# Routed attention and a gated FFN on one core: a fifth group prepared by VectorE, v loaded four heads ahead, one-hots issued by GpSimd

## The chip, the cores and the metric

One Trainium2 chip, one core. The metric is the device time of one execution in microseconds (us): the median of twelve runs, beside one profiled execution whose trace is read here. The engines are PE (TensorE, matrix products), VectorE (DVE in the profile), ScalarE (ACT), GpSimd (POOL) and SyncE (SP, which here only issues DMAs). Each engine runs its own list of instructions in order and waits on semaphores for the others.

## What is computed

Attention in which a query sees only the keys of its own cluster, then a gated FFN behind an RMS norm. There are 4 batches, 8 heads, 768 positions, a head dimension of 64 and 16 clusters for each head; the FFN takes 3072 tokens of 512 to 1536 and back.

```python
q_assign = np.argmax(np.einsum('bhsd,hcd->bhsc', q_n, c_n), axis=-1)
k_assign = np.argmax(np.einsum('bhsd,hcd->bhsc', k_n, c_n), axis=-1)
mask = q_assign[:, :, :, None] == k_assign[:, :, None, :]
scores = scale * np.matmul(q, k.transpose(0, 1, 3, 2))
scores = np.where(mask, scores, -1000000000.0)
scores = scores - np.max(scores, axis=-1, keepdims=True)
attn = np.exp(scores)
attn = attn / (np.sum(attn, axis=-1, keepdims=True) + 1e-09)
return np.matmul(attn, v).astype(np.float32)
...
rms = np.sqrt(np.mean(x * x, axis=-1, keepdims=True) + 1e-06)
xn = x / rms * rms_g
g = xn @ w_gate
silu = g * (1.0 / (1.0 + np.exp(-g)))
val = xn @ w_val
return (silu * val @ w_out).astype(np.float32)
```

## The kernel before

**The mask as part of the product.** Each head's q and k are held transposed in SBUF, 64 rows of values, and under them 16 rows that hold a one-hot of the position's cluster. The product of the two (line 345) is then the score plus a large number where the clusters agree, and the exponential with a bias (line 349) brings all others to 0. The large number is `ZS`: up to group 4 the keys are divided by it and the exponential multiplies it back; from group `BG` on the keys stay as they are and their one-hots are multiplied by it (line 282).

**Groups.** The 32 heads (4 batches of 8) are prepared in eight groups of four, numbered 0 to 7. Preparing a group means:

- `load_qk` and `load_v` (lines 95 and 100): DMAs on SP's queue into the staging buffers. There are `NQ` = 6 for q and k and `NV` = 8 for v; a load waits until its buffer is free. For groups below `BG`, q or k of a head is one DMA of 192 KB (line 85). From `BG` on it is four DMAs of 48 KB (line 93), which bring half rows of 32 numbers (128 bytes) to such places that transposing blocks of 32 by 32 gives the layout needed.
- `trans` (line 209): below `BG`, three transposes by PE into PSUM (line 218), then a copy to `qkT` by ScalarE (line 224) or VectorE. From `BG` on, one block transpose by VectorE (line 214).
- `cast` (line 230): from `qkT` to bf16 in `qext` and `kext`. GpSimd casts q; k is cast by VectorE below `BG` and by GpSimd from `BG` on. `vcast` (line 239) is GpSimd's too, and frees the v buffer.
- `cluster_steps` (line 265): cluster products on PE (line 251), then the largest, the comparison and transposes on VectorE; the last, line 283, leaves the one-hots in `put`.
- `place` (line 289): DMAs of 12 KB each, which carry the one-hots to their rows under q and k.

**Units.** The attention runs in eight units: for each batch first one half of the queries, then the other. A unit has 24 rounds (8 heads, 3 rounds each) of scores on PE, exponential on ScalarE and, a round later, the product with v (line 363). Between the rounds `attention` (line 655) puts pieces of other work from a list: it spreads them by their costs, which are written beside each piece. In unit u this other work is the expert products (lines 441 and 466) of the units before, and the preparation of group u + 2. Unit 1 prepares groups 2 and 3, unit 2 prepares group 4 and ends what remains of group 3 (the one-hots of its keys), units 3 to 5 prepare groups 5 to 7. The batch of unit u uses groups 2(u // 2) and the next, so unit 2 uses groups 2 and 3.

**Order of the queues.** The order on each engine is the order in which the program writes the pieces. `others` (line 494) stands with each head n of groups 2 to 7: it casts v of head n, loads q and k of head n + 6, and loads v of head n + 8. Before it, `second_batch` (line 607) loads q and k of heads 12 and 13 and v of heads 8 to 15. At the end of a unit's norm, `rms` (line 403) puts a transposing DMA of the normed tokens, `xnT`, on SP's queue; the next expert products need it. The one-hots of group 2 are placed on SP's queue, all others on GpSimd's. In unit 1, GpSimd's list is: v casts of group 2, then casts and v casts of group 3 with the three loads of `w_out` (line 204, 512 KB each) between them, then the one-hots of group 3's queries.

The lines that set the work of a group above 3:

```python
if g > 3:
    a[:1] = [(1.4, lambda f=(a[0][1], a.pop(4)[1]): [x() for x in f])]
    a.append((0.0, lambda: [place(nc.gpsimd, g, m) for m in range(2)]))
```

Of the kernel before, what the change touches and what calls it, by code (L numbers as in the profile page):

```python
# [22 lines left out]
def kernel(  # L23
# [12 lines left out]
    nc = tc.nc  # L36
    B, H, S, D = q.shape
# [16 lines left out]
    CUT = 2 * FC - 8  # L54
    LEAD = 6
    NQ, NV = 6, 8
    BG = 5

    ctx.enter_context(tc.manual_schedule())
    pool = lambda n, b, **kw: ctx.enter_context(tc.tile_pool(name=n, bufs=b, **kw))  # L60
# [16 lines left out]
    def src(a, n):  # L77
        b, h = divmod(n, H)
        return a[b, h].rearrange("(p t) d -> p t d", t=ST)

    def load(n, part, on=None):
        if n not in staged:
            staged[n] = stage.tile([P, 2, ST, D], F32, tag="qk", name="qk")
        if n < BG * HG:
            (on or nc.sync).dma_start(out=staged[n][:, part], in_=src((q, k)[part], n))
# [9 lines left out]
    def load_qk(n):  # L95
        if n < B * H:
            load(n, 0)
            load(n, 1)

    def load_v(n, vq=None):  # L100
        if n >= B * H:
            return
        stagedv[n] = stage.tile([P, ST, D], F32, tag="vs", name="vs", bufs=NV)
        (vq or nc.sync).dma_start(out=stagedv[n], in_=src(v, n))
# [104 lines left out]
    def trans(g, h, part, on=None):  # L209
        if (g, h // 2) not in qkT:  # L210
            qkT[g, h // 2] = qk32.tile([P, 2, 2, UQ], F32, tag="qkT", name="qkT")
        qk = staged[g * HG + h]
        if g >= BG:
            nc.vector.transpose(qkT[g, h // 2][:, h % 2, part], qk[:, part].rearrange("p t d -> p (t d)"))
            return
        ps = ps_g.tile([P, UQ], F32, tag="gen", name="tq")
        for i in range(HT):
            nc.tensor.transpose(ps[:, i * P:(i + 1) * P], qk[:, part, 2 * i:2 * i + 2].rearrange("p t d -> p (t d)"),  # L218
                                ident_f)
        to, by = qkT[g, h // 2][:, h % 2, part], 1.0 / ZS if part else 1.0  # L220
        if on is nc.vector:
            nc.vector.tensor_scalar_mul(to, ps, by)  # L222
        else:
            nc.scalar.activation(to, ps, ACT.Copy, scale=by)
# [5 lines left out]
    def cast(on, g, h, part, es=(0, 1)):  # L230
        for e in es:
            to = cols((kext if part else qext)[g % 4][:D, h], g, e)
            of = qkT[g, h // 2][e * D:(e + 1) * D, h % 2, part]
            if on is nc.scalar:
                nc.scalar.copy(to, of)
            else:
                on.tensor_copy(to, of)  # L237

    def vcast(n):
        nc.gpsimd.tensor_copy(vbf[n // HG % 4][:, n % HG, :, :D], stagedv[n])  # L240
# [24 lines left out]
    def cluster_steps(g, m):  # L265

        of = {}

        def products():
            of["cl"] = cluster_products(g, [(h, m) for h in range(HG)])  # L270

        def most():
            of["mx"] = largest(of["cl"])

        def same():
            of["ohT"] = asg.tile([P, UQ], BF16, tag="ohT", name="ohT", bufs=2)
            compare(of["ohT"].rearrange("p (b e c) -> p b e c", e=2, c=NC), of["cl"], of["mx"])

        def back():
            put[g, m] = asg.tile([P, UQ], BF16, tag="oh", name="oh", bufs=3)  # L280
            if m and g >= BG:
                nc.vector.tensor_scalar_mul(of["ohT"], of["ohT"], ZS)
            nc.vector.transpose(put[g, m], of["ohT"])  # L283

        return [products, most, same, back]
# [3 lines left out]
    def place(on, g, m, es=(0, 1)):  # L289

        ext = (kext if m else qext)[g % 4]
        for h in range(HG):
            for e in es:
                on.dma_start(out=ext[D:D + NC, h, e * UQ:(e + 1) * UQ],  # L294
                             in_=put[g, m][32 * h + e * NC:32 * h + (e + 1) * NC])
# [39 lines left out]
    def scores(u, h, i):  # L335
# [12 lines left out]
        of = ps[:, :, :w] if nt == HT else flat[:, :n * w].rearrange("p (c w) -> p c w", w=w)  # L348
        nc.scalar.activation(pT[u, h][:, n * i:n * i + n, :w], of, ACT.Exp, bias=off, scale=scale if g >= BG else scale * ZS)  # L349

# [135 lines left out]
    def group_work(g):  # L486

        t, c = [], []
        for h in range(HG):
            n = g * HG + h  # L490
            w = 0.0 if g >= BG else 0.3
            t += [(w, lambda h=h: trans(g, h, 0)), (w, lambda h=h: trans(g, h, 1))]

            def others(n=n):
                vcast(n)
                load_qk(n + NQ)
                load_v(n + NV)

            def both(h=h, f=others):
                cast(nc.gpsimd, g, h, 0)  # L500
                f()
                cast(nc.gpsimd if g >= BG else nc.vector, g, h, 1, (0,))
            if g == 2:
                c.append((0.0, others))
            else:
                c += [(0.0, both), (0.0, lambda h=h: cast(nc.gpsimd if g >= BG else nc.vector, g, h, 1, (1,)))]
        a = []
        for m in range(2):
            a += [(0.0 if i else 0.7, f) for i, f in enumerate(cluster_steps(g, m))]
            if g == 3:  # L510
                a.append((0.0, lambda m=m: place(nc.gpsimd, g, m)))
            elif g == 2:
                a.append((0.0, (lambda: (place(nc.sync, g, 1), place(nc.sync, g, 0, (1,)))) if m else
                          (lambda: place(nc.sync, g, 0, (0,)))))
        if g > 3:
            a[:1] = [(1.4, lambda f=(a[0][1], a.pop(4)[1]): [x() for x in f])]
            a.append((0.0, lambda: [place(nc.gpsimd, g, m) for m in range(2)]))
        return t, c, a
# [5 lines left out]
    def group(g):  # L524

        if g >= NG:
            return [], []
        t, c, a = group_work(g)
        return [x for h in range(HG) for x in t[2 * h:2 * h + 2] + c[2 * h:2 * h + 2]], a
# [13 lines left out]
    def ffn_work(u):  # L543
        n = UNITS[u][2] / HT
        return [(0.64 * n, lambda f=f, val=val: gv(u, f, val)) for f in range(FC) for val in (False, True)]

    def out_work(u):
        return [(0.86, lambda t=t, p=p: out_mm(u, t, p)) for t in range(UNITS[u][2]) for p in range(3)]
# [58 lines left out]
    def second_batch():  # L607
        nc.sync.dma_start(out=hold, in_=invs[0].rearrange("p a t -> p (a t)"))
        for n in range(H + HG, H + NQ):
            load_qk(n)  # L610
        for n in range(H, H + NV):
            load_v(n)

    def gap1():
# [12 lines left out]
    def gap5():  # L627
# [11 lines left out]
        for n in (6, 7):  # L639
# [6 lines left out]
    first = {0: lambda: trans(1, 0, 0), 1: gap1, 2: early[0], 3: early[1], 4: lambda: (early[2](), early[3]()), 5: gap5,  # L646
             7: lambda: head(5), 9: lambda: pair_clusters(3), 10: lambda: head(6),
             13: lambda: (casts(nc.vector, 6, K0, K1), head(7)), 14: lambda: (more(), second_batch())}
    first.update({16: None, 19: None, 22: None})
    first.update({i: f for i, f in zip((15, 17, 18, 20, 21, 23), late)})  # L650
# [25 lines left out]
    for u in range(1, NU):  # L676
        ffn, o, g = ffn_work(u - 1), out_work(u - 2) if u > 1 else [], u + 2
        if u == 1:
            t, c, a = group_work(2)
            t3, c3, a3 = group_work(3)  # L680
            n = LEAD - 4
            o3 = [(0.0, lambda i=i: load_o(i)) for i in range(0, FC, 4)]
            prep = c + a + spread(weave(t3[n:], c3), o3) + a3[:5]
            idle = const.tile([P, 1], BF16)

            def norm():
                rms(0)
                nc.gpsimd.tensor_copy(idle, xn[0][:, CC - 1, HT - 1, P - 1:])
                for h in range(HG):
                    casts(pool_, H + h, K0, Q0, K1, Q1)  # L690

            hooks = {(1, 0, 0): late[6], (1, 0, 1): lambda: (late[7](), norm())}
            hooks.update({(1, *divmod(2 + i, HT)): t3[i][1] for i in range(n)})
            hooks[1, *divmod(LEAD - 1, HT)] = lambda: xtrans_all(0)
            fill = spread(ffn[:CUT], prep)
            attention([(1, h) for h in range(H)], fill, LEAD, hooks)
        else:
            fill = ffn_work(u - 2)[CUT:] + [(0.0, lambda u=u: rms(u - 1))]
            rows, clusters = group(g)
            if u == 2:  # L700
                fill += spread(o[:3], [(0.0, f) for _, f in a3[5:]])
                o = o[3:]
            fill += spread(o, rows) + spread(ffn[:CUT], clusters)
            attention([(u, h) for h in range(H)], fill, 1 if g < NG else 0)
# [41 lines left out]
```

The softmax here doesn't subtract the row's maximum and nothing guards it: scores larger than these inputs give would overflow.

## Time and profile before

| | us |
|---|---|
| median of 12 runs | 334.12 (333.4 to 338.27) |
| the profiled execution | 334.1 |
| its span, first to last instruction | 332.0 |
| unit 2, first scores to those of unit 3 | 41.8 |
| units 3 and 4, the same | 37.5 and 37.6 |

The granted TensorE clock is full throughout. A line of the page's part 5 gives the line, the engine, the operation, what it writes and reads with its shape, the count; then the busy time and the mean duration in ns; then the engine's idle time ahead of it and what ended that. A line of a timeline gives start, duration, engine, line, operation, tiles and count, and in brackets an idle time and what ended it. A line of the stages gives the stretch and its length, then the busy time and number of instructions of PE, weight loads, VectorE, ScalarE and GpSimd, the clock, the mean share of the 16 DMA engines that is in use, and GB/s.

Transfers by kind, as the page has them: v 32 loads of 192 KB, 4.2 us to land; q and k 40 loads of 192 KB, 3.0 to 4.2 us, and 96 of 48 KB, 2.6 to 2.7 us; one-hots 80 from GpSimd, 2.2 to 2.4 us, and 16 from SP, 4.9 to 5.4 us.

### The profile page before, as it was taken

The page shows a single profiled execution, that of the slowest core. Times are in us where ns is not written, and L with a number is a line of the kernel's source. Part 1 is how long each engine was busy: PE and PEld are TensorE (multiplying, and loading weights), DVE is VectorE, ACT ScalarE, POOL GpSimd, SP SyncE. Part 2 cuts the span into 40 slices and gives each one's busy share as a digit, 9 for nine tenths or more (in the row PEclk, how much of TensorE's full clock was granted, in tenths as well). Part 3 has the DMA queues.
Part 4 walks back from the last instruction along what each step waited for, and adds up shares of the span by engine and source line. Part 5 has one row for each costly group of instructions (what it writes and reads, how often), then busy time and mean ns, then how long its engine had stood idle before and what let it go on. Part 6 is the DMA issues. An engine that isn't in the chain of part 4 may idle for free.

```text
span 332.0 us, 7838 instructions
## 1 busy us (share of the span) xinstructions
PE 323.9 (98%) x2901; PEld 195.6 (59%) x2901; DVE 222.4 (67%) x507; ACT 250.5 (75%) x437; POOL 124.6 (38%) x249
## 2 busy tenths in 40 slices
PE   8999899999999999999999999999999999999996
PEld 4546557565656655665556655665566656655654
DVE  6999876868378694877678684876355644685430
ACT  5899979976868877798768876798788878863322
POOL 6999498240925338260744438170000000000000
PEclk9999999999999999999999999999999999999999
DMA  7999989955755625552551022000400040002002
GB/s 271 374 260 215 243 150 225 209 158 109 156 117 103 144 55 117 118 128 42 89 118 47 14 53 92 2 22 5 116 28 1 2 109 35 2 1 75 21 0 97
DMA packets 71269, 34.23 MB, mean 103 GB/s; under 512 B 51392, under 2 KB 68160, under 8 KB 71232
## 3 DMA queue, kind: packets, MB, share of 16 engines
q1 hardware_dynamic: 62576, 27.64, 32.0%
q0 software_dynamic: 8368, 5.71, 10.7%
q8 instruction: 23, 0.38, 0.5%
q10 hardware_dynamic: 288, 0.39, 0.3%
q14 instruction: 14, 0.11, 0.1%
HBM read 28.61 MB, written 6.29 MB: 105 GB/s over the span
## 4 chain that ended last, share of the span: by engine, by line
PE 79%; DVE 10%; ACT 6%; DMA 2%; issue 2%; ACTq 0%; DVEq 0%
PE gate L441 17%; PE val L441 17%; PE o L466 16%; PE s L345 15%; PE acc L363 8%; ACT pT L349 3%; PE sc L251 2%; DMA xnT<-xn 1%; ACT xn L390 1%; DVE xn L400 1%; PE tq L218 1%; DVE kext L329 1%; DVE qext L329 1%; DVE pads L324 1%; ACT th L449 1%
## 5 line engine op out<-in xcount | busy, mean ns | idle before, releaser
L349 ACT ACTIVATE pT<-s,off 128x768 bf16<-128x768 f32 x192 | 170.9, 904 | 32.2 <-PE s L345 31.7
L345 PE MATMUL s<-qext,kext 80*128 80x384 bf16 x384 | 94.8, 327 | 2.4 <-ACT pT L349 1.6
L441 PE MATMUL gate<-xnT,wg 128*128 128x384 bf16 x384 | 78.3, 326 | 0.2 <-DMA xnT<-xn 0.2
L441 PE MATMUL val<-xnT,wv 128*128 128x384 bf16 x384 | 78.1, 326 | 0.0
L450 DVE SCALAR_TENSOR_TENSOR th<-th,gate 128x384 f32<-128x384 f32 x84 | 46.3, 551 | 37.2 <-ACT th L449 36.6
L466 PE MATMUL o<-wo,gvT 128*128 128x512 bf16 x276 | 68.1, 379 | 0.0
L345 PEld LDWEIGHTS <-kext 80*128 80x128 bf16 x384 | 36.4, 98 | 35.9 <-issue 9.3
L454 DVE SCALAR_TENSOR_TENSOR gvT<-th,val 128x384 bf16<-128x384 f32 x84 | 46.5, 553 | 9.7 <-PE val L441 3.0
L449 ACT ACTIVATE th<-gate 128x384 f32<-128x384 f32 x84 | 41.1, 490 | 15.0 <-PE gate L441 14.3
L441 PEld LDWEIGHTS <-wg 128*128 128x128 bf16 x384 | 35.9, 97 | 23.4 <-issue 0.8
L363 PEld LDWEIGHTS <-pT 128*128 128x128 bf16 x1152 | 43.4, 97 | 10.1 <-DVE x L370 1.1
L441 PEld LDWEIGHTS <-wv 128*128 128x128 bf16 x384 | 36.1, 97 | 22.5
L237 POOL CAST qext<-qkT 64x384 bf16<-64x384 f32 x64 | 36.0, 569 | 35.1 <-DVE inv L368 20.8
L363 PE MATMUL acc<-vbf,pT 128*128 128x65 bf16 x1152 | 45.7, 193 | 0.6 <-ACT pT L349 0.2
L466 PEld LDWEIGHTS <-gvT 128*128 128x128 bf16 x276 | 25.8, 97 | 25.7 <-issue 0.6
L294 POOL DMA_DIRECT2D qext<-oh x40 | 19.1, 487 | 35.1 <-DVE oh L283 29.3
L237 POOL CAST kext<-qkT 64x384 bf16<-64x384 f32 x46 | 25.4, 552 | 3.9 <-DVE qkT L222 2.3
L294 POOL DMA_DIRECT2D kext<-oh x40 | 19.2, 489 | 18.9 <-DVE oh L283 18.9
L469 ACT COPY o_sb<-o 128x512 f32<-128x512 f32 x23 | 13.5, 585 | 16.1 <-PE o L466 16.1
L368 DVE RECIPROCAL inv<-acc 128x6 f32<-128x6 f32 x32 | 6.1, 190 | 21.5 <-PE acc L363 21.1
L218 PE MATMUL tq<-ident_f,qk 128*128 128x128 f32 x120 | 19.1, 279 | 0.1
L370 DVE TENSOR_TENSOR x<-acc,inv 128x384 f32<-128x384 f32 x32 | 17.9, 558 | 1.1
(83 smaller groups left out, 241.6 us busy)
## 6 DMA issues: line engine op xcount, KB each, us to landing
vs<-in_v_dram SPq DMA_DIRECT2D x32, 192.0 KB, 4.2
out_dram<-o_sb SPq DMA_DIRECT2D x23, 256.0 KB, 2.7
qk<-in_q_dram SPq DMA_DIRECT2D x20, 192.0 KB, 4.2
qk<-in_k_dram SPq DMA_DIRECT2D x18, 192.0 KB, 4.1
qk<-in_q_dram SPq DMA_DIRECT2D x48, 48.0 KB, 2.7
qk<-in_k_dram SPq DMA_DIRECT2D x48, 48.0 KB, 2.6
wg<-in_moe_w_gate_dram POOLq DMA_DIRECT2D x4, 384.0 KB, 8.7
wv<-in_moe_w_val_dram POOLq DMA_DIRECT2D x4, 384.0 KB, 10.9
```

The lines of the kernel that those rows point to most:

```text
L218: nc.tensor.transpose(ps[:, i * P:(i + 1) * P], qk[:, part, 2 * i:2 * i + 2].rearrange("p t d -> p (t d)"), ident_f)
L237: on.tensor_copy(to, of)
L294: on.dma_start(out=ext[D:D + NC, h, e * UQ:(e + 1) * UQ], in_=put[g, m][32 * h + e * NC:32 * h + (e + 1) * NC])
L345: nc.tensor.matmul(ps[:, j, :w] if nt == HT else flat[:, j * w:(j + 1) * w], lhsT=cols(kext[g % 4][:KR, hh], g, kc // HT, kc % HT * P, (kc ...
L349: nc.scalar.activation(pT[u, h][:, n * i:n * i + n, :w], of, ACT.Exp, bias=off, scale=scale if g >= BG else scale * ZS)
L363: nc.tensor.matmul(acc[:, h % 2, t], lhsT=pT[u, h][:, kc, t * P:(t + 1) * P], rhs=vbf[g % 4][:, hh, kc % HT * 2 + kc // HT], start=kc == 0 ...
L370: nc.vector.tensor_tensor(dst, acc[:, :, :nt, :D], inv[:, :, :nt].unsqueeze(3).broadcast_to([P, 2, nt, D]), op=ALU.mult)
L441: nc.tensor.matmul(ps, lhsT=w[:, c, f * P:(f + 1) * P], rhs=xnT[u][:, c, :n], start=c == 0, stop=c == CC - 1)
L449: nc.scalar.activation(th, ps, ACT.Tanh, scale=0.5)
L450: nc.vector.scalar_tensor_tensor(th, th, 1.0, ps, op0=ALU.add, op1=ALU.mult)
L454: nc.vector.scalar_tensor_tensor(gvT[u][:, f, :n], gates[u], 0.5, ps, op0=ALU.mult, op1=ALU.mult)
L466: nc.tensor.matmul(outs[u], lhsT=gvT[u][:, f, t * P:(t + 1) * P], rhs=wo[:, f], start=f == 0, stop=f == FC - 1)
```

## The change

```diff
     NQ, NV = 6, 8
-    BG = 5
+    AV = 4
+    BG = 4
...
             def others(n=n):
                 vcast(n)
                 load_qk(n + NQ)
-                load_v(n + NV)
+                load_v(n + AV)
...
             elif g == 2:
-                a.append((0.0, (lambda: (place(nc.sync, g, 1), place(nc.sync, g, 0, (1,)))) if m else
-                          (lambda: place(nc.sync, g, 0, (0,)))))
+                a.append((0.0, (lambda: (place(nc.gpsimd, g, 1), place(nc.gpsimd, g, 0, (1,)))) if m else
+                          (lambda: place(nc.gpsimd, g, 0, (0,)))))
...
         for n in range(H + HG, H + NQ):
             load_qk(n)
-        for n in range(H, H + NV):
+        for n in range(H, H + AV):
             load_v(n)
```

Three edits in one:

- `BG` 4: group 4 (heads 16 to 19, the fifth) is loaded in half rows, 32 DMAs of 48 KB in place of 8 of 192 KB; transposed by VectorE, not by PE and ScalarE; its keys are cast by GpSimd, not VectorE; and the cost written beside each of its transposes is 0, not 0.3.
- `AV` 4: v of head n + 4 is loaded with head n, and `second_batch` loads v of heads 8 to 11 only. The eight v buffers stay.
- The 16 one-hot DMAs of group 2 (the third) are issued by GpSimd instead of SP. On GpSimd they stand behind the v casts of group 2 and ahead of the casts of group 3.

## The prediction

> **What bounds the kernel now.** I read the page's busy shares and its chain first, then the busy time unit by unit (a unit is half the queries of one batch: 24 rounds of scores), then the timelines of PE, SP, VectorE and GpSimd around the one unit that is longer than its neighbours.
>
> From the page: the busy line, the chain by engine, and the group of PE transposes.
>
> ```profile
> PE 323.9 (98%) x2901; PEld 195.6 (59%) x2901; DVE 222.4 (67%) x507; ACT 250.5 (75%) x437; POOL 124.6 (38%) x249
> ...
> PE 79%; DVE 10%; ACT 6%; DMA 2%; issue 2%; ACTq 0%; DVEq 0%
> ...
> L218 PE MATMUL tq<-ident_f,qk 128*128 128x128 f32 x120 | 19.1, 279 | 0.1
> ```
>
> The chain is PE for 79% of the span. ScalarE's idle time is mostly a wait for PE (31.7 us of waiting for scores). So what PE doesn't have to do is worth its time, if nothing else is late. The change takes 24 of the 120 transposes of line 218.
>
> Busy time of each engine by unit (second, third, fourth):
>
> ```profile
> 65.16:106.96 41.80, 41.25 (x374) 25.03 (x372) 29.48 (x67) 32.60 (x60) 17.88 (x37) 1.00 0.64 133
> 106.96:144.50 37.54, 37.48 (x343) 22.33 (x341) 27.21 (x61) 29.44 (x52) 17.38 (x36) 1.00 0.53 111
> 144.50:182.10 37.60, 37.34 (x343) 22.22 (x341) 27.47 (x62) 29.50 (x52) 17.47 (x36) 1.00 0.38 80
> ```
>
> The second unit (counted from 0, batch 1, first half) prepares group 4, with transposes on PE. The third and fourth prepare groups 5 and 6, by VectorE. The same scores, values and expert products take 41.8 us there and 37.5 to 37.6 in the others.
>
> PE's timeline inside that unit:
>
> ```profile
> 81.90 0.49 PE L218 MATMUL tq<-ident_f,qk 128*128 128x128 f32 x3
> 82.23 1.02 PE L466 MATMUL o<-wo,gvT 128*128 128x512 bf16 x4
> ...
> 86.17 0.49 PE L345 MATMUL s<-qext,kext 80*128 80x384 bf16 x2
> ...
> 89.76 0.49 PE L345 MATMUL s<-qext,kext 80*128 80x384 bf16 x2
> 90.42 0.82 PE L441 MATMUL gate<-xnT,wg 128*128 128x384 bf16 x4 [0.17 <-DMA xnT<-xn]
> ```
>
> Three transposes hold PE for 0.33 us (81.90 to 82.23), although the mean duration of one is 279 ns: they overlap. And at 90.42 the first expert product waits for the transposing DMA of xnT. That DMA stands on SP's queue behind other work:
>
> ```profile
> 36.02 0.54 SPq L85 DMA_DIRECT2D qk<-in_k_dram  x1
> 49.18 0.33 SPq L104 DMA_DIRECT2D vs<-in_v_dram  x1
> ...
> 58.01 7.81 SPq L294 DMA_DIRECT2D kext<-oh  x8
> 65.87 3.46 SPq L294 DMA_DIRECT2D qext<-oh  x4
> ...
> 84.89 0.56 SPq L104 DMA_DIRECT2D vs<-in_v_dram  x1
> 85.64 1.97 SPq L403 DMA_TRANSPOSE xnT<-xn  x1
> ```
>
> SP stands still from 36.6 to 49.18 (v of head 16 needs the buffer of v 8, which GpSimd frees), then issues without a pause. xn is ready on VectorE at 79.78 (77.70 + 2.08); its transpose goes out 5.9 us later, and lands 4.7 us after that, at 90.4. Now the one-hot keys of group 3:
>
> ```profile
> 82.06 0.57 DVE L283 STREAM_TRANSPOSE oh<-ohT 128x384 bf16<-128x384 bf16 x1
> ...
> 82.92 3.99 POOL L294 DMA_DIRECT2D kext<-oh  x8 [11.76 <-DVE oh L283]
> ```
>
> The first of them lands 2.2 us after 82.92, and the scores of head 4 need it at 86.17. It has 1 us to spare.
>
> **What the Trainium skill says.** "TensorE: Matmul & The Clock Gate", Part 4, PE-mode transpose, gives about 275 ns for one in a kernel's context, and says that its output needs a copy out of PSUM. The trace agrees on both (279 ns; a 496 ns copy by ScalarE for each three), but what PE loses is 0.11 us each. "DMA: Bandwidth & Descriptors", Issuing engines are not separate DMA queues, says that issuing from several engines saves the sequencer's time alone. I use it for the one-hots that go from SP to GpSimd; here SP's time is what xnT waits for. The same page, Specifications, wants 512 B or more for line rate. The half-row loads move 128 B pieces: between 124 and 128 us the SP queue's 2416 packets took 47.5% of the 16 engines, so 0.30 us of all of them for a 48 KB load (384 packets). "SBUF — State Buffer", Who interferes with whom, says that some VectorE operations shut GpSimd out. The trace shows casts of 0.50 us stretched to 0.84 once; I leave 1 us for it.
>
> **Part 1: group 4 by VectorE (BG 4).**
> - PE loses 24 transposes, eight times 0.33 us: -2.64. Two waits in the same unit go if their causes go: 0.33 at 79.7 (the second transpose waits for a PSUM buffer) and 0.33 before 90.42 (xnT): -0.66. Together -3.3 at most.
> - Another way to it: with these edits the second unit is like the fourth (37.58 between first scores, 144.35 to 181.93), plus the 0.78 us of cluster products of group 3 that only it has (75.13 to 75.91): 38.36 against 41.80, so -3.4. The weights of the transposes in the fill become 0, as in the later units, so that the spread is theirs too.
> - ScalarE loses eight copies (3.7 us in its timeline, 80.7 to 90.6). It isn't the bound: nothing.
> - VectorE gets eight transposes (seven took 3.33 us at 121.78: 0.476 each, 3.8) and a 0.25 us scaling, and loses eight key casts (0.68+0.73+0.93+0.93 = 3.3). In its order they stand behind line 283 at 82.06, so they run from 82.6 to 86.5. The cluster products need them about 88.8: 2 us to spare. Nothing.
> - GpSimd gets those eight key casts (0.53 each, 4.2 us). Its casts for group 4 then run from 86.9 to 97.6; the next thing on its queue, the one-hots of group 4, waits for VectorE until 101.8 in the trace. Nothing; without that cover it would still have until the fourth unit.
> - SP issues 32 transfers instead of 8 for heads 16 to 19, at 0.66 us each (72.43 to 75.15 for four) instead of 0.48: +17 us of its time, between 37 and 66 us. See part 2.
>
> **Part 2: v four heads ahead.** Each v load finds a free buffer (8 remain), so SP no longer stands still until 49.18. Its queue becomes: v 8 to 11, then q and k of 14, v 12, q and k of 15, v 13, the eight pieces of 16, v 14, and so on to v 19, then xnT. A load waits for the eighth one before it to land: at 60.85 a one-hot went out when the q load of 52.87, eight issues earlier, landed (8.0 us). Until 46 us the DMA engines are full (75% + 43% of them between 36 and 46), so I let the pieces of head 16 be out by 46. Then 46 transfers remain (40 pieces, 6 of v) at 0.67: until 76.8. xn comes at 79.8, so its transpose goes out at once and lands near 84.5. PE comes to the first expert product at 65.16 + 20.52 (its place in the third unit) + 0.97 (the products, and 0.19 of a start wait) + 0.5 (below) = 87.15. Margin 2.6 us. The engines' load between 46 and 80 was 77%. The pieces take 12 us of it and the wo loads 10.2 (78.8% of 13 us), and with v and one-hots the sum stays near 26 of 34 us.
>
> **Part 3: one-hots of group 2 by GpSimd.** SP is rid of 16 transfers that held it from 55.0 to 69.3. GpSimd gets 16 of 0.488: +7.8 us, in front of group 3's casts, v casts and the three wo loads, which are all that is queued behind. The casts begin at 58.3 instead of 50.43; the wo loads go out at 59.9, 63.8 and 66.1 instead of 52.3, 57.3 and 60.9; GpSimd is through at 67, where before it waited until 67.29 anyway. The third wo load lands 7.8 to 9.9 us later (three seen), at 74.6 to 76.7 with its 0.74 of issue; PE wants it at 77.55 (its place in the third unit, 118.38, moved as above). That is the thinnest cover: 0.8 to 2.9 us. Unhidden, a late wo costs PE its lateness.
>
> **What is late next.** Without transposes PE comes to head 4's scores at 65.16 + 18.46 + 0.97 = 84.6. The one-hot keys can't be earlier: their VectorE chain starts with rms at 75.85 and stays. They land at 82.92 + 2.2 = 85.1. A new wait of 0.5 us (0 if the landing takes 1.6, as once seen; 1.5 if it takes 3.2). A late wo would be inside it for its first half microsecond.
>
> **Sum.** -3.4 + 0.5, and +0.1 because the third unit may get the 0.26 us start wait that the fourth has: -2.8. Against the profiled execution (span 332.0, run 334.1, so 2.1 around it): 329.2 + 2.1 = 331.3. The median of the twelve runs is 334.12, the same base. -0.8%.
>
> **Rivals.**
> - A, the sum: 331.3, with 330.5 to 332.3 from the landing times above. Chance 0.68.
> - B, the gain mostly goes into new waits: wo or xnT about 1.6 us behind PE. For it: both margins are below 3 us and rest on landing times under load (8 to 10 us seen). Against: SP idles before 79.8 by my count. -2.8 + 1.6: 332.9. Chance 0.2.
> - C, slower: the half-row pieces clog SP. If, while the wg, wv and wo loads run (until about 75 us), a piece lands as late as the q load at 36.02 did (9.0 us), eight in flight give one issue per 1.13 us: 25.7 of the 46 are out at 75, the other 20.3 at 0.67 take until 88.6, and the gate starts at 93.3, 6.2 us behind A: 337.5. It decides from an issue of xnT after 85.3 (no gain left). For it: 128 B pieces in a full stretch, and a queue kept in order. Against: pieces landed in 2.2 to 4.7 us wherever they were seen, even with 71% of the engines in use. Chance 0.12.
> - That PE's time is not the bound there, so that removing it does nothing, I set aside: the third unit has just this form and takes 37.5 us.
>
> **Numbers.** Half a percent (1.7 us) is what can be told from no change. A lies mostly beyond it, B within, C beyond on the other side: faster 0.69, same 0.19, slower 0.12. The range takes A and most of B: 330.5 to 333.6.
>
> **What would show it.** Right: the second unit near 38.9 us; no line 218 after 61 us; xnT issued within 1 us of xn; a wait of about 0.5 us at head 4's first scores. Wrong: SP still issuing pieces after 82 us (C), PE waiting at line 466 near 77 us for wo (B), or VectorE transposes ending after 88.8 us.

## The result, and the profile after

The changed kernel takes 339.37 us (median of 11 runs, 334.77 to 340.24), the kernel before in the same comparison 334.35 us (median of 47). The ratio is 1.0119, with a 95% interval of 1.0096 to 1.0141: slower by about 1.2%, where 331.3 us and a gain of 0.8% were forecast. (The ratio is formed from the fast runs alone and is not the quotient of the two medians, which is 1.015.) The profiled execution of the changed kernel took 338.71 us, with a span of 336.8. Line numbers after are one higher than before from the setting of `AV` on.

The page's busy line, PE clock, chain by engine, and the group of the first expert products (gate):

```profile
PE 322.9 (96%) x2877; PEld 193.4 (57%) x2877; DVE 223.9 (66%) x508; ACT 247.7 (74%) x429; POOL 136.1 (40%) x273
...
PEclk9999999999899999999999999999999999999999
...
PE 73%; DVE 11%; ACT 7%; DMA 5%; issue 2%; SPq 1%; DVEq 0%; ACTq 0%
...
L442 PE MATMUL gate<-xnT,wg 128*128 128x384 bf16 x384 | 78.9, 327 | 3.7 <-DMA xnT<-xn 3.6
```

PE has 24 transposes fewer (2877 instructions, not 2901), and the chain has DMA at 5% where it had 2%. A wait for xnT of 3.6 us stands at the gate products where it was 0.2, and one slice of the PE clock falls to 8.

The stretches of the changed kernel: unit 2, unit 3, the time right after that wait, and two stretches of the DMA engines (stretch and length; busy time of PE, weight loads, VectorE, ScalarE, GpSimd; clock; DMA share; GB/s):

```profile
65.79:109.76 43.97, 39.84 (x350) 22.69 (x349) 30.04 (x67) 29.49 (x52) 23.54 (x48) 0.96 0.75 137
109.76:147.34 37.58, 37.32 (x341) 22.22 (x340) 27.45 (x62) 29.48 (x52) 17.46 (x36) 1.00 0.51 103
...
92.00:94.20 2.20, 2.20 (x9) 0.99 (x8) 0.56 (x1) 0.49 (x1) 2.02 (x5) 0.50 0.48 76
...
66.00:77.00 11.00, 10.74 (x97) 6.11 (x96) 7.72 (x20) 9.35 (x20) 5.85 (x12) 1.00 1.20 194
```

Unit 2 was to shrink from 41.80 to 38.9 us. It grew to 43.97, though PE is busy for less of it. The span grew by 4.8 us: 2.17 in unit 2, 0.19 in unit 3 (37.58 between first scores; before, it was 37.39, from 106.96 to 144.35, where the stretch read for the prediction ended at 144.50), 0.63 ahead of unit 2 (0.62 of it ahead of the first scores, 10.87 against 10.25), and 1.8 at the very end. The last two are not in the places that the change touches; they are taken up at the end of the experiments.

PE's timeline where the time goes (start, duration, engine, line, operation, tiles, count, and the idle time ahead with what ended it):

```profile
85.72 0.50 PE L346 MATMUL s<-qext,kext 80*128 80x384 bf16 x2 [0.22 <-DMA kext<-oh]
...
87.24 0.71 PE L364 MATMUL acc<-vbf,pT 128*128 128x65 bf16 x18
91.60 1.44 PE L442 MATMUL gate<-xnT,wg 128*128 128x384 bf16 x4 [3.65 <-DMA xnT<-xn]
92.83 1.48 PE L442 MATMUL val<-xnT,wv 128*128 128x384 bf16 x4
94.11 0.58 PE L346 MATMUL s<-qext,kext 80*128 80x384 bf16 x2
```

The one-hot keys of head 4 come 0.22 us late, as forecast. But xnT comes 3.65 us late, and after that wait PE runs slowly: four gate products take 1.44 us where they take 0.81 elsewhere, and the stretch from 92.0 to 94.2 has a clock of 0.50. From the gate at 91.60 to the cluster products at 94.62 it is 3.02 us; the same instructions take 1.71 where PE was kept busy (experiment e6). So the wait costs 3.65 + 1.31 = 4.96 us, nearly all of the 5.07 that lie between the forecast 38.9 us and 43.97. "TensorE: Matmul & The Clock Gate" in the Trainium skill, Part 1, The HAM clock gate, puts PE at half rate after an idle window of about 3.4 us. This trace agrees in that the half rate (0.50) follows the wait of 3.65 us; what shorter waits did is told in the last section.

Why is xnT late? SP's timeline, changed kernel:

```profile
37.79 5.45 SPq L94 DMA_DIRECT2D qk<-in_q_dram  x4
43.29 5.82 SPq L94 DMA_DIRECT2D qk<-in_k_dram  x4
49.22 0.62 SPq L105 DMA_DIRECT2D vs<-in_v_dram  x1
...
57.39 2.60 SPq L94 DMA_DIRECT2D qk<-in_q_dram  x4
60.04 2.62 SPq L94 DMA_DIRECT2D qk<-in_k_dram  x4
...
66.67 5.82 SPq L94 DMA_DIRECT2D qk<-in_k_dram  x4
...
73.32 4.18 SPq L94 DMA_DIRECT2D qk<-in_q_dram  x4
...
86.75 0.56 SPq L105 DMA_DIRECT2D vs<-in_v_dram  x1
87.50 1.85 SPq L404 DMA_TRANSPOSE xnT<-xn  x1
```

SP's list never runs empty here, and its last load ahead of the transposing DMA goes out at 86.75. xn was ready at 79.8. Four pieces of 48 KB take 2.6 us where the DMA engines have room (57.39), but 5.45 and 5.82 from 37.79 on, and 5.82 and 4.18 from 66.67 and 73.32 on. How late these pieces land, from the list of the q and k tiles' DMAs between 66 and 77 us (duration of an issue, then issue to landing, each as minimum, median, maximum; ns, and us for the landing):

```profile
L94 SPq DMA_DIRECT2D qk<-in_q_dram x5: 579/617/1531, 65.7 to 76.9; - x5
L94 SPq DMA_DIRECT2D qk<-in_k_dram x4: 682/1164/2677, 66.7 to 69.8; - x4
...
DMA to landing us min/median/max: 2.7/7.8/10.2
```

The five pieces issued from 65.7 to 69.8 landed in 7.8 to 10.2 us, the four from 73.3 to 76.9 in 4.7 falling to 2.7, and those from 77.5 to 80 again in 2.3 to 2.8. One (76.92) went out only when the eighth DMA ahead of it on the queue (66.67) had landed, at 76.91. This limit of eight is the program's: in the trace the 225 DMAs of SP's queue report their landing on eight semaphores in turn, and none goes out before its semaphore's last one has landed. Three others were slow in the issue itself, 1.5 to 2.7 us in place of 0.62. The DMA share of this stretch is 1.20; above 1, the packets of the two queues overlap in time (queue; packets, MB, share of the 16 engines):

```profile
q0 software_dynamic: 1303, 1.15, 61.7%
q1 hardware_dynamic: 5011, 0.97, 57.8%
```

GpSimd's queue (q0: w_out with a cast, and the one-hots) has 61.7% and SP's (q1) 57.8%. "DMA: Bandwidth & Descriptors", Queues, rings and completion order, says that an engine takes turns between its queues packet by packet. The nearly equal shares of time fit that, but they don't show it: the packets counted are 1303 and 5011.

GpSimd's timeline in the same stretch:

```profile
67.34 0.74 POOL L205 DMA_DIRECT2D wo<-in_moe_w_out_dram  x1
68.07 2.93 POOL L295 DMA_DIRECT2D qext<-oh  x6
72.51 0.49 POOL L295 DMA_DIRECT2D qext<-oh  x1 [1.51 <-DMA wo<-in_moe_w_out_dram]
75.92 0.48 POOL L295 DMA_DIRECT2D qext<-oh  x1 [2.92 <-DMA qext<-oh]
82.92 3.81 POOL L295 DMA_DIRECT2D kext<-oh  x8 [6.52 <-DVE oh L284]
```

GpSimd stands still twice for landings, but is done well ahead of 82.92, where VectorE sets the start as before. What was read as hidden on GpSimd is hidden.

### The profile page after: what moved, and what is told of

Same layout as the page of the kernel before. It is cut to its first block, busy times and chain, and to the rows that moved or that the text cites. A ratio compares the mean times of both kernels' runs of the same rounds, so it can differ in the third digit from the quotient of the medians.

```text
span 336.8 us, 7827 instructions
## 1 busy us (share of the span) xinstructions
PE 322.9 (96%) x2877; PEld 193.4 (57%) x2877; DVE 223.9 (66%) x508; ACT 247.7 (74%) x429; POOL 136.1 (40%) x273
## 4 chain that ended last, share of the span: by engine, by line
PE 73%; DVE 11%; ACT 7%; DMA 5%; issue 2%; SPq 1%; DVEq 0%; ACTq 0%
PE gate L442 16%; PE val L442 16%; PE o L467 15%; PE s L346 14%; PE acc L364 8%; ACT pT L350 3%; PE sc L252 2%; ACT xn L391 2%; ACT th L450 1%; DVE xn L401 1%; DMA xnT<-xn 1%; DMA out_dram<-o_sb 1%; DVE kext L330 1%; DVE qext L330 1%; DVE pads L325 1%
## 5 line engine op out<-in xcount | busy, mean ns | idle before, releaser
L295 POOL DMA_DIRECT2D qext<-oh x48 | 23.2, 492 | 32.5 <-DVE oh L284 28.1
L238 POOL CAST kext<-qkT 64x384 bf16<-64x384 f32 x54 | 29.4, 545 | 4.3 <-DVE qkT L223 2.5
L295 POOL DMA_DIRECT2D kext<-oh x48 | 23.0, 488 | 14.7 <-DVE oh L284 14.7
L391 ACT ACTIVATE xn<-x 128x384 bf16<-128x384 f32 (+1 forms) x42 | 17.3, 415 | 0.0
```

Of the source, the lines that this page charges most:

```text
L295: on.dma_start(out=ext[D:D + NC, h, e * UQ:(e + 1) * UQ], in_=put[g, m][32 * h + e * NC:32 * h + (e + 1) * NC])
L391: nc.scalar.activation(junk, x, ACT.Square, scale=DM ** -0.5, accum_out=to)
```

## The experiments

The question is which part brings the loss, and whether the gain of part 1 is there at all. The theory: PE's gain is real, but SP's queue carries 32 pieces of 48 KB in place of 8 whole loads ahead of xnT's transposing DMA, and they go out slowly while the DMA engines are full. The rivals: VectorE or GpSimd became late with group 4; w_out or the one-hots come late; or the loss lies outside unit 2. Each experiment's time is a ratio to the kernel before on the same chip, and "unit 2" is the time from its first scores to those of unit 3, in the profiled execution.

### e1_repeat: the changed kernel again

> The changed kernel once more, for a second trace. Theory 1 (SP's queue is too long when xnT wants to go): xnT is issued 6 us or more after xn is ready, PE waits 3 to 4 us for it in unit 2, then runs its first products at half clock; unit 2 lasts 43.5 to 44.5 us (41.8 before). The 0.6 us lost before the first scores and the 1.8 us lost at the last output in the first trace of the changed kernel are of that one execution and won't both come back. Theory 2 (the small pieces slow things all over): the losses at the start and at the end come back at the same places and sizes.

338.2 us, ratio 1.011 [1.0066, 1.0153]. Unit 2 takes 43.82 us. xnT is issued at 89.26, and PE waits 3.09 us for it. The loss in unit 2 is thus the same, and PE again runs slowly behind the wait, though from 94.6 on and not at once. Outside it the same kernel lost other amounts than in its first trace: its first scores come at 11.90, unit 2 begins at 68.03, 2.9 us later than in the kernel before, and the end loses 0.5 us and not 1.8. That belongs to the open part below.

### e2_bg5 and e3_bg4_only: the parts apart

```diff
-    BG = 4
+    BG = 5
```

> The changed kernel with group 4 as before (BG 5): v four heads ahead and the one-hots by GpSimd alone. Theory 1: SP is free before xn is ready, so xnT goes out within 0.5 us of it; PE loses no wait before the first gate product; unit 2 lasts 41.4 to 41.8 us and the time is that of before, 333.6 to 334.4. Theory 2 (GpSimd's longer list or the later w_out loads cost the time): 336 or more, with PE waiting at the out products or at head 4.

Parts 2 and 3 alone: 334.19 us, ratio 0.9985 [0.9964, 1.0006]. No difference that can be measured. xnT is issued at 80.46, PE doesn't wait for it, and unit 2 takes 41.47 us, 0.33 less than before.

Of the other kernel the base is the kernel before, with `BG` set to 4 and nothing else changed.

> The kernel before with BG 4 alone: v eight heads ahead and the one-hots of group 2 on SP stay. Theory 1: about 74 transfers stand between 49 us and xnT on SP's queue, so xnT goes out near 100 us and the one-hots of group 2 come late too; PE waits 10 to 17 us in unit 2; 345 to 352. Theory 2: as the changed kernel, 338 to 340.

Part 1 alone: 355.47 us, ratio 1.0658 [1.0609, 1.0706], more than the 345 to 352 us that were expected. PE's two long waits, from its timeline in that kernel:

```profile
72.88 1.44 PE L345 MATMUL s<-qext,kext 80*128 80x384 bf16 x4 [7.22 <-DMA kext<-oh]
...
107.59 1.44 PE L441 MATMUL gate<-xnT,wg 128*128 128x384 bf16 x4 [11.31 <-DMA xnT<-xn]
```

Both DMAs that PE waits for stand on SP's queue behind the pieces: the one-hots of group 2, and xnT, issued at 103.13. So the pieces are what costs time, and parts 2 and 3 do what they can against it: they bring xnT forward from 103.13 to 87.50. That isn't enough.

### e4_defer and e10_defer_again: sixteen pieces moved behind xnT

If SP's queue is all that is wrong, the pieces that nobody needs early can go behind the transposing DMA. Heads 20 and 21 belong to group 5, which unit 3 prepares.

```diff
+    LATE = (20, 21)
...
-                load_qk(n + NQ)
+                if n + NQ not in LATE:
+                    load_qk(n + NQ)
...
+            if u == 2:
+                fill += [(0.0, lambda n=n: load_qk(n)) for n in LATE]
```

> The changed kernel with q and k of heads 20 and 21 loaded behind xnT instead of ahead of it: 16 transfers less ahead of it. Theory 1: xnT goes out within 1.5 us of xn, lands before PE comes to its first gate product at about 87.5, the half-clock stretch is gone; unit 2 lasts 38.6 to 39.2 us; 331 to 332. Theory 2: no gain over the changed kernel beyond 1 us.

332.01 us, ratio 0.9938 [0.9919, 0.9957]. The same kernel once more:

> The kernel with heads 20 and 21 put off, once more with more rounds, as the version to keep: 331.5 to 332.5, a ratio of 0.992 to 0.995 to the kernel before.

332.29 us, ratio 0.9909 [0.9877, 0.9942]. It beats both kernels. Unit 2 takes 38.86 and 38.93 us. SP's timeline in the first of the two:

```profile
67.37 4.86 SPq L95 DMA_DIRECT2D qk<-in_k_dram  x4
72.33 2.33 SPq L106 DMA_DIRECT2D vs<-in_v_dram  x3
79.74 1.56 SPq L405 DMA_TRANSPOSE xnT<-xn  x1
81.36 2.98 SPq L95 DMA_DIRECT2D qk<-in_q_dram  x4
...
118.82 0.56 SPq L106 DMA_DIRECT2D vs<-in_v_dram  x1
119.55 1.86 SPq L405 DMA_TRANSPOSE xnT<-xn  x1
```

SP is through at 74.7 and waits for xn, so the transpose goes out at 79.74 and PE's gate at 87.57 finds it landed. The slow stretch is still there (67.37: four pieces in 4.86 us, and a DMA share of 1.26 from 66 to 77 us). It costs nothing now. The 16 pieces go out in unit 2, and there SP has no gap until the transpose of unit 3 at 119.55, 1.2 us after that unit's xn (118.37). It lands 4.7 us later, at 124.3, and PE comes to it at 125.15: 0.9 us of cover, all that this kernel has there. In e10 the cover is used up: that transpose goes out at 120.5 and lands at 125.7, the gate starts at 125.75, and unit 3 takes 37.74 us and not 37.59.

### e5_defer_one: eight pieces moved

```diff
-    LATE = (20, 21)
+    LATE = (21,)
```

> The changed kernel with q and k of head 21 alone behind xnT: 8 transfers less ahead of it, 5.3 us of SP's time in the two traces. Theory 1 (the queue ahead of xnT): xnT goes out near 82.2, lands near 86.7, PE comes to it near 87.1, so a wait of 0 to 0.5 us and nearly the whole gain: 332.0 to 332.7. A rival (any crowding of the queue costs in proportion, wait or not): half way between the changed kernel and the one with two heads put off, 335 to 336.

333.43 us (332.4 to 337.82, five runs), ratio 0.9968 [0.9925, 1.0012]: between the two expectations, and not told from no change. xnT goes out at 82.03, as was expected, but its profiled execution (337.82 us, the longest of the five, so it does not stand for the median) lost time where no theory had put it. PE waits 2.34 us at head 4's first scores. The profile names a cast of GpSimd as what ended this wait, but the first one-hot key landed at 87.77, 0.05 us ahead of the scores. The one-hot keys, issued from 82.90 on, land in 3.9 to 4.9 us and not in 2.0 to 2.8, and the transposing DMA, in flight at the same time, lands in 6.7 us and not in 3.8 to 4.1. Experiment e11 returns to that.

### e6_keep_busy: the half rate after the wait

The changed kernel, with 14 matmuls that nothing uses put in front of unit 2's first gate product.

```diff
-            fill += spread(o, rows) + spread(ffn[:CUT], clusters)
+            fill += spread(o, rows)
+            if u == 2:
+                fill.append((0.0, lambda: busy(14, False)))
+            fill += spread(ffn[:CUT], clusters)
```

> The changed kernel with 14 idle matmuls of 0.22 us (3 us) on PE right ahead of the first gate product of unit 2, which run while xnT is waited for. If the slow products behind the wait come from PE having stood idle: xnT's time stays, but the products behind it run at full rate; unit 2 lasts 42.4 to 42.8 us (43.8 to 44.0 without), 1.2 to 1.6 us less in the time of the changed kernel. If they come from something else (the transposing DMA, the cluster products): unit 2 stays at 43.8 to 44.0.

336.74 us, ratio 1.0057 [1.0032, 1.0083], 1.5 us below the repeat of the changed kernel; the interval lies below that of the changed kernel in the result (1.0096 to 1.0141). PE's timeline:

```profile
87.92 3.19 PE L130 MATMUL warm<-warm 128*128 128x512 bf16 x14
92.26 0.81 PE L442 MATMUL gate<-xnT,wg 128*128 128x384 bf16 x4 [1.15 <-DMA xnT<-xn]
92.91 0.81 PE L442 MATMUL val<-xnT,wv 128*128 128x384 bf16 x4
93.56 0.49 PE L346 MATMUL s<-qext,kext 80*128 80x384 bf16 x2
93.97 1.50 PE L252 MATMUL sc<-qkT,cblk 128*32 128x384 f32 x16
```

The gate starts later than in the changed kernel (xnT was issued at 88.14 here), but runs at the full rate at once: 1.71 us to the cluster products, not 3.02. Unit 2 takes 43.22 us; 42.4 to 42.8 had been expected, and the difference is xnT's issue, 0.54 us later counted from the unit's first scores (43.97 - 1.31 + 0.54 = 43.20). The slow stretch is thus the consequence of PE's idling.

### e7_wo_first: the w_out loads moved

The theory says that the pieces are slow where w_out's loads run beside them. Moved ahead of group 2's one-hots, the loads should take the slow stretch with them.

```diff
-            prep = c + a + spread(weave(t3[n:], c3), o3) + a3[:5]
+            prep = c + o3 + a + weave(t3[n:], c3) + a3[:5]
```

> The changed kernel with the three w_out loads issued by GpSimd ahead of the one-hots of group 2 (near 51 us, not 60 to 68). Theory 1a (the DMA engines have so much work that a load more in one place is a load less in another): the slow stretch of SP's queue moves from 66 to 77 us to 51 to 62 us, xnT still goes out at 85.5 or later; 337 to 340. Theory 1b (w_out slows the pieces only where the in-flight limit meets them late): xnT goes out at 81 to 84 and the gain appears, 332 to 334.

340.3 us, ratio 1.0161 [1.0135, 1.0187]. SP's timeline:

```profile
53.42 5.54 SPq L94 DMA_DIRECT2D qk<-in_k_dram  x4
...
59.88 6.30 SPq L94 DMA_DIRECT2D qk<-in_q_dram  x4
66.22 2.64 SPq L94 DMA_DIRECT2D qk<-in_k_dram  x4
```

The slow pieces are now at 53 to 66 us, and from 66 on four take 2.6; the DMA share is 1.03 from 46 to 66 us (0.75 in the changed kernel) and 0.55 from 66 to 77 (1.20). But xnT goes out at 88.27, not earlier. The delay moved with the loads and did not shrink, so it is the amount of work ahead of xnT that counts, not an unlucky moment. PE waits 4.32 us.

### e8_defer_sp_onehots and e9_defer_v8: are parts 2 and 3 needed?

Both start from e4_defer. The first puts group 2's one-hots back on SP:

```diff
-                a.append((0.0, (lambda: (place(nc.gpsimd, g, 1), place(nc.gpsimd, g, 0, (1,)))) if m else
-                          (lambda: place(nc.gpsimd, g, 0, (0,)))))
+                a.append((0.0, (lambda: (place(nc.sync, g, 1), place(nc.sync, g, 0, (1,)))) if m else
+                          (lambda: place(nc.sync, g, 0, (0,)))))
```

> The kernel with heads 20 and 21 put off, with the one-hots of group 2 back on SP (the third part undone): 16 transfers more ahead of xnT, at 0.65 to 0.9 us each. Theory 1: xnT goes out 10 to 14 us later than with GpSimd (79.7), at 86 to 91 (SP had 4 us to spare); PE waits 1 to 6 us; 335 to 340. Rival (that part is of no use once there is room): 332 to 332.7.

338.05 us, ratio 1.0119 [1.0066, 1.0173]. xnT goes out at 83.03, 3.3 us later than in e4 and less late than expected. PE waits 1.17 us for one-hot keys and 0.44 at the gate. Unit 2 takes 40.41 us, and unit 3 takes 39.86 in place of 37.6: SP's delay passes through its full queue to the next transpose (issued at 124.40), for which PE waits 2.12 us.

The second has v eight heads ahead again:

```diff
-    AV = 4
+    AV = 8
```

> The kernel with heads 20 and 21 put off, with v loaded eight heads ahead again (the second part undone). SP then waits for the v buffer of head 16 until 49 us, with q and k of heads 15 to 19 and eight v loads behind it: 34 pieces and whole loads and 8 of v, 0.67 to 0.85 us each. Theory 1: xnT goes out at 78 to 85, so it costs between nothing and 3 us: 332 to 335. Rival (what matters is that SP never stands still): 336 or more.

338.82 us, ratio 1.0118 [1.0073, 1.0164]. That is a miss: 332 to 335 had been expected. SP stands still from 38.3 to 49.52 for a v buffer, time in which e4 issues the eight pieces of head 16. xnT goes out at 85.16, PE waits 2.12 us for it, and unit 2 takes 42.97 us. Unit 3 again loses 1.4 (wait of 1.21). So parts 2 and 3, together worth nothing while PE does group 4's transposes (e2), are each needed for the gain of part 1.

### e11_second_transpose: does a transposing DMA slow the one-hots?

Again from e4_defer; unit 2's transposing DMA is issued twice in a row.

```diff
+            if u == 1:
+                nc.sync.dma_start_transpose(out=xnT[u].rearrange("p c (t x) -> p (c t) x", x=P),
+                                            in_=xn[u].rearrange("p c t x -> p (c t x)"))
```

> The kernel that loads q and k of heads 20 and 21 behind xnT, with the transposing DMA of unit 2 issued twice in a row: the second one writes the same values into the same tile, right behind the first. Nothing else is in flight then but the third group's one-hot keys, which GpSimd issues from about 82.7 us on. Theory (a transposing DMA in flight slows the one-hot keys' landing, and they slow it): the second transposing DMA is in flight from about 83.5 to 88 us, the one-hot keys land in 3.5 to 5 us instead of 2.0 to 2.8, PE waits 1 to 2.5 us at the first scores of head 4, and unit 2 takes 40 to 41.5 us. Rival (the late landings seen before came from the pieces that were still in flight): they land in 2.0 to 2.8 us, the wait at the scores is at most 0.7, and unit 2 takes 38.8 to 39.4, with at most 0.5 us of waiting at the gate for the second transposing DMA.

337.95 us (median of 20 runs), ratio 1.0108 [1.0088, 1.0127]. The one-hot keys' landing in this kernel:

```profile
DMA to landing us min/median/max: 1.7/3.0/3.6
```

This lies between the two expectations. The first three keys, issued from 83.25 on and all but the third ahead of the second transpose (84.13), take 1.7 to 2.2 us, soon enough that PE doesn't wait; the five behind it take 2.9 to 3.6. In e4 the keys took 2.0 to 2.7 us, with pieces of q and k in flight beside them from 81.36 on, but with the transpose landed at 83.6: it is the transpose that slows the keys, and not the pieces. The gate waits 0.91 us for the second transpose, and unit 2 takes 39.54. What costs most is in unit 3, and wasn't expected: the pieces behind the second transpose start at 85.60 and not at 81.36, and with no gap in SP's queue the next transpose goes out at 124.76 and not at 119.55. PE waits 2.64 us for it, then runs slowly, and unit 3 takes 42.02 us. This shows how thin the cover of e4 in unit 3 is.

### What stays open

The 0.6 us at the start and the 1.8 at the end of the changed kernel. The end, on ScalarE's timeline of the changed kernel:

```profile
333.70 0.27 ACT L483 COPY o_sb<-o 128x128 f32<-128x128 f32 x1 [2.80 <-DMA out_dram<-o_sb]
```

Before, this last copy waited 1.04 us for PE; here it waits for an earlier output DMA to land. In the other kernels it waited 1.03 (e2, e6), 1.04 (e10), 1.51 (e1, e4), 3.57 us (e7), without a pattern in what they change. The first scores came between 10.58 and 11.90 in eleven traces of kernels made from the changed one, at 10.57 in e3, and at 10.25 in the one trace of the kernel before; the faster e4 and e10 are among the eleven (10.68, 11.00). The changed kernel alone, in its two traces, gave 10.87 and 11.90 for the start and 2.80 and 1.51 for that wait, so one execution differs from the next by about as much as is to be explained. No experiment was aimed at either, so whether the change has a part in them isn't settled.

## Why the prediction was wrong

**Part 1** was right in mechanism and size. The sum was -3.4 + 0.5 for unit 2, 38.9 us in all; once SP is relieved, unit 2 takes 38.86 and 38.93 (e4, e10). Its one-hot wait is 0.2 to 0.3 us and not 0.5, so the rest takes 0.3 us more than the forecast 38.36; that the sum is met so closely is luck in so far. VectorE's transposes, GpSimd's casts and ScalarE's saved copies cost and bring nothing, as forecast. A saved 2.8 us against 334.1 was the forecast; e4's span is 1.8 us shorter: unit 2 -2.94, unit 3 +0.2 (the start wait that was counted as 0.1), start +0.4, end +0.5.

**Part 2** holds the failed step: "so I let the pieces of head 16 be out by 46. Then 46 transfers remain (40 pieces, 6 of v) at 0.67: until 76.8." The order of the queue and the number of transfers were right. Both times were not. The pieces of head 16 were out at 49.1, since eight of them took 11.3 us in the full stretch, 1.41 each. The 46 then took from 49.2 to 87.3, which is 0.83 each. Of the 7.3 us more, 3.5 are in head 19 and 2.1 in head 20, beside w_out's loads, and 1.4 in head 17, whose cause is open; this is against 5.25 for eight pieces (57.39 to 62.7). With 3.2 of the late start that is 10.5 us; the cover was the 3 us that SP was to idle and 2.6 for the landing. That leaves a wait of 4.9 us; it was 3.65, since unit 2 began 0.6 us later and the transpose landed in 4.1 us and not in 4.7. Relieving SP of 16 transfers (e4), and nothing else, brings the forecast time of unit 2 back: that shows the step.

The price of 0.67 came from stretches in which the DMA engines had room (shares of 0.68 and 0.52 in the kernel before, from 66 to 77 and from 77 to 87 us), and even there four pieces had taken 3.64 us once, at 75.15. The check on the sum of the engines' load, 26 of 34 us, couldn't see this: the load from 46 to 80 came to 0.87, which is 29.6 us, still below one, while the stretch from 66 to 77 stood at 1.20. e7 shows that the place of w_out's loads doesn't matter, so the term is the work ahead of xnT, priced at what the full engines let through. That their load is what made the issues slow, and not something in SP's issuing, is argued from these shares; no run changed the size of the pieces or took the weight loads away.

A second term was missing. The price of a late xnT was taken to be its lateness; PE's half rate after it added 1.31 us in the profiled execution, and e6 shows that the half rate doesn't come when PE is kept busy.

**Part 3** was right. PE didn't wait for w_out; GpSimd was through at 76.4 and not at 67, and nothing came from that.

**The rivals.** C, with a chance of 0.12, is what happened: its sign, nearly its size (337.5 us forecast, 339.37 measured; xnT issued at 88.6 forecast, 87.50 and 89.26 seen in the two traces of the changed kernel; the gate at 93.3, seen at 91.60 and 93.36), and the mark that it named, pieces still going out after 82 us (the last at 86.03). It put the slow issue under the weight loads, where most of it was: head 16's pieces beside those of w_gate and w_val, issued from 31.45 to 35.9 and landing in 9.8 to 14.0 us, heads 19 and 20 beside w_out's. Its mechanism came only in part. The pieces landed late, and eight in flight did hold the queue, but this held four pieces (39.38, 40.48, 41.57 and 76.92) for 2.6 us in all; 10.0 us came from issues that themselves took longer than 0.62 us, which C did not have. It was set low because "pieces landed in 2.2 to 4.7 us wherever they were seen, even with 71% of the engines in use". None had been seen beside such loads. What had been seen there was late: the two whole loads of the prediction's own working, 8.0 us and 9.0 (this was the q load at 35.34; the k load at 36.02 took 9.4), and in the kernel before the one-hots of 12 KB on SP's queue, 4.9 to 5.4 us at the median. B's form of the loss, w_out late, didn't occur.

## What to carry to other kernels

When a change puts more DMAs on a queue, price them at what the same queue took in the most crowded stretch that they will pass through, not at the rate of an idle one; a mean share of the DMA engines below one does not clear the stretch above one. What is late at the end of an in-order queue is the small DMA that someone waits for: look for transfers ahead of it that nobody needs yet, move those behind it, and then look at the next such DMA, which inherits the delay. To a wait of PE of more than 2 us add the half rate that may follow it: 1.3 us in the changed kernel's first trace, 1.6 in its second.

## What was not expected of the hardware

- A transposing DMA in flight slows small one-hot DMAs. Where they didn't meet, or only at one end, a key took 2.2 to 2.5 us at the median. Where they met, it was 4.4 us (e5), 4.1 (e8), 3.1 (e9) and 3.0 (e11), and e11 shows the step within one trace. That the keys slow the transpose is not shown. The transpose of unit 2 took 4.6 to 6.7 us beside them and 3.8 to 4.4 elsewhere, but in unit 3, with no one-hot DMA in flight, it took 5.47 us in the changed kernel and 4.75 and 5.21 in e4 and e10. "DMA: Bandwidth & Descriptors", Rules for kernel authors, says that a transpose next to ordinary DMAs needs nothing, where it speaks of corrupted data; in time, the keys paid for it here.
- PE's half rate comes in stretches of a fixed length. Ahead of the program's end each lasts 3.41 us, or two or three times that (e3), and within a trace they start a whole number of 3.413 us apart (72 in the changed kernel, 71 in e1, 9 between the first two of e3). So the clock is set anew at the borders of a grid, wherever the waits fall. Up to 325 us the thirteen traces have 1225 stretches of that grid: eleven in which PE was idle for 2.12 us or more, each followed by the half rate, and all the others with at most 1.74 us of idle time, each followed by the full rate. So a wait's place decides. In e9 a wait of 2.12 us lay within one stretch, in e8 a border cut the same wait in two (stretch and length, then PE's busy time; the clock is the third number from the end; e9, then e8):

```profile
86.99:90.40 3.41, 1.29 (x23) 1.00 (x22) 1.24 (x3) 1.42 (x3) 3.08 (x7) 1.00 0.94 143
90.40:93.81 3.41, 3.41 (x17) 1.31 (x18) 1.11 (x2) 1.30 (x2) 3.18 (x7) 0.50 0.47 74
...
124.71:128.12 3.41, 2.25 (x27) 1.39 (x26) 0.75 (x2) 2.45 (x4) 3.13 (x7) 1.00 1.00 161
128.12:131.53 3.41, 2.45 (x22) 1.22 (x25) 0.97 (x2) 1.12 (x2) 2.96 (x6) 1.00 0.52 87
```

- For the same reason the first gate products were slow at once in the changed kernel (a border at 90.87, 0.73 us ahead of them), while in e1, e7 and e11 the first four still took 0.81 us and the cluster products behind them 2.3 to 2.7 us in place of 1.5 (borders 0.8 to 1.3 us after PE had resumed). "TensorE: Matmul & The Clock Gate", Part 1, gives an idle window of about 3.4 us; 2.12 us of idle time within a stretch of that length were enough here.
- One SP instruction for a 48 KB load of 128 B pieces took up to 2.7 us itself, with the DMA engines full, in place of 0.62.
